# Reordering the second, third and fourth head groups of a fused attention and maxout kernel: loads, casts, masks and value products

## The chip, the cores and the metric

The kernel runs on one core of one Trainium2 chip. A core has five engines that run side by side, each through its own queue in order: TensorE (PE, matrix products; its weight loads are shown as PEld), VectorE (DVE), ScalarE (ACT), GpSimd (POOL) and SyncE (SP). SP, ACT and POOL also issue DMA transfers; those that POOL issues go through one queue (q0, "software"), those of SP through another (q1). The metric is the time of one execution on the device, in microseconds (us); lower is better. Seven runs of the kernel before the change gave a median of 258.22 us, from 257.61 to 260.21.

## What is computed

Blockwise causal attention feeds a maxout layer.

```python
B, H, S, D = 8, 8, 576, 64; block = 64
scores = (q @ k.transpose(0, 1, 3, 2)) / sqrt(D)
scores = where(block_i >= block_j, scores, -1e9)     # by blocks of 64 positions
attn = softmax(scores)
x = (attn @ v).transpose(0, 2, 1, 3).reshape(4608, 512)
g = maximum(x @ w1, x @ w2)                          # w1, w2: 512 x 1024
out = g @ w_out                                      # w_out: 1024 x 512
```

All inputs and the output are float32; the kernel works in bf16 with float32 accumulation.

## The kernel before

**Pairs and groups.** Two heads with the same place in their pair of heads are handled together as a *pair* p (32 pairs, four to a batch), since 64 rows of head dimension fill half of TensorE's rows. Two pairs make a *group* g (16 groups, two to a batch). Groups 0 and 1 are a hand-written start with their own tiling; group 2 is written out by hand too; groups 3 to 15 run in a loop. The change touches group 2 and the first turns of the loop (groups 3 and 4).

**One group.** `load_qk` brings q and k of the group as float32 (SP issues the DMA; a one-element memset on POOL, the "gate", stands before it and holds it until POOL gets there). `cast` turns them into bf16. `transposes` turns them on TensorE into PSUM and returns a function that copies the result out (two copies, one for each pair, on the engines named). `pad_keys` (POOL) prepares a copy of some keys for the corner blocks. Then for each pair three tiles of scores: `tile_0`, `tile_1`, `tile_2` write scores into one of two PSUM buffers (`ps_s`), and return a function that takes the exponential on ACT (1024 columns each, tile_2 with a small second one) into `aT` and sets the masked corners to zero with memsets on POOL (`mask`). `region` calls these functions. With two buffers, the scores of a tile wait for the exponential of the tile before the last one.

**Values.** `av(p, ts)` multiplies the exponentials of a pair with V (`ps_o`), and DVE divides by the sums (reciprocal and multiply) into `xp`. `av_with(p, n)` does it in two parts with n steps of other work between. V of a batch comes in five chunks, `load_v(b, c)`, issued by POOL. `x_out(g)` transposes a group's values into `xT` (two copies); for groups from 4 on a DMA does this instead. When the second group of a batch is through, `done_tokens` rises, and more of the second layer may run.

**The second layer.** max(x w1, x w2) is computed as max(x (w1 - w2), 0) + x w2. `diff_w(j)` is the subtraction for a quarter of the columns on DVE (it needs `load_w1(j)`, 512 KB, and `load_w2(j)`, both issued by POOL). The second part times w_out is one matrix, M = w2 w_out, which the kernel computes itself (`bT_unit`, `m_unit`). `h_unit(i, f)` is one block of 128 hidden columns for a span of 512 tokens (four matmuls, then DVE's maximum with 0 into `g`); columns f = 0 and 1 need `diff_w(0)`, 2 and 3 `diff_w(1)`, and so on. `y_unit` makes 128 rows of output (twelve matmuls, a DVE copy, a store by SP).

**Fill.** All these are units in one list, and `fill(n)` puts the next n steps of them (a 512-column matmul is one step, a 256-column one a half) into TensorE's queue between the parts of attention. `fill_of(g)` says how many steps a group gets: what is ready, less KEEP = 14, divided by the groups left until more becomes ready.

**What sets the order.** Every engine runs its instructions in the order in which the program writes them; there is no scheduler. Four PSUM buffers (`ps_m`) serve transposes, M, h, y and the values; two (`ps_s`) the scores. Raw q and k have three buffers each, the bf16 copies two, `aT` four (one a pair). `pool_work(s)` is called at the end of a pair's turn in the loop: the loads of the group after next but one, the casts of the group after next, the V chunks of the next batch.

**Around the change, in the order written (line numbers of the kernel before):** the second part of the start issues `load_w1(0)` and the load of group 2 (625, 626), `load_w1(1)`, `load_w1(2)` (636, 637), `load_w1(3)` (646), the casts of group 2 and the load of group 3 (647 to 649) and V's first chunk (650); group 2 is transposed (656, 657), scored (663, 667, 671) and masked tile by tile, with the other V chunks and `diff_w` between; then come the casts of group 3 (673, 674), its transposes (679, 682), and the loads of groups 4 and 5 with the casts of group 4 (`pool_work(4)`, `pool_work(5)`). In the loop the values of pair p - 2 run in the turn of pair p.

Of the kernel before, what the change touches and what calls it, by code (L numbers as in the profile page):

```python
# [14 lines left out]
def kernel(  # L15
# [12 lines left out]
    B, H, S, D = q.shape  # L28
    P = 128
    BLK = 64  # L30
    HP = H // 2
# [367 lines left out]
    def exp(p, ps, w, a0):  # L399
        nc.scalar.activation(  # L400
            out=aT_r[p % NA][:, :, a0:a0 + w], in_=ps[:, :, :w], func=AF.Exp, scale=scale,
        )
# [36 lines left out]
    def tile_0(p):  # L439
        u = ps_s.tile([P, 2, 512], FP32, name="ps_s", tag="s")  # L440
        scores(p, u, 0, 0, 0, 512)
        return lambda: (exp(p, u, 512, 0), mask(p, 0))

    def tile_1(p):
        u = ps_s.tile([P, 2, 512], FP32, name="ps_s", tag="s")
        scores(p, u, 0, 0, 512, 64)
        scores(p, u, 64, 1, 128, 448)
        return lambda: (exp(p, u, 512, 512), mask(p, 576))

    def tile_2(p):  # L450
        u = ps_s.tile([P, 2, 512], FP32, name="ps_s", tag="s")
        corner_scores(p, u, 320)
        scores(p, u, 0, 2, 256, 320)
        scores(p, u, 384, 3, 448, P)

        def out():
            exp(p, u, 512, 1024)
            nc.scalar.activation(  # L458
                out=aT_r[p % NA][BLK:, :, 1536:AW], in_=u[BLK:, :, 320:320 + BLK],
                func=AF.Exp, scale=scale,  # L460
            )
            mask(p, 1024)
            mask(p, 1344)
        return out

    def region(*tiles):
        for out in tiles:
            out()

    def av(p, ts):  # L470
        b, hp = divmod(p, HP)
# [75 lines left out]

    def pool_work(s):
        g, i = divmod(s, 2)
        if s == 4:  # L550
            load_qk(4, (SP, SP), gated=True)
        elif s == 5:
            load_qk(5, (SP, SP), gated=True)
            cast("q", 4, ((pool, 0, RPP),))
            cast("k", 4, ((pool, 0, RPP),))
        else:
            if i == 1 and g + 3 < NG:
                load_qk(g + 3, (SP, SP), gated=True)
            if i == 1 and g + 2 < NG:
                cast("q", g + 2, ((pool, 0, RPP),))  # L560
                cast("k", g + 2, ((pool, 0, RPP),))
            nb, j = divmod(s + 2, HP)
            if nb < B:
                for c in ((0, 1), (2, 3), (4,), ())[j]:
                    load_v(nb, c)
            for nm in "qk":
                if i == 1 and g + 3 < NG and by_dma(nm, g + 3):
                    load_blocks(nm, g + 3)
# [65 lines left out]
    burst_q3(2)  # L634
    masks_q(2)
    load_w1(1)
    load_w1(2)
    fill(2)
    burst_q1(3)
    fill(2)  # L640
# [2 lines left out]
    av(2, [2, 3, 4])  # L643
    burst_q3(3)
    masks_q(3)
    load_w1(3)
    cast("q", 2, ((pool, 0, RPP),))
    load_qk(3, (SP, SP), gated=True)
    cast("k", 2, ((pool, 0, RPP),))
# [4 lines left out]
    x_out(1, 0, NCH, (act, act))  # L654
    fill(4)
    transposes("q", 2, (dve, act))()
    transposes("k", 2, (dve, act))()
    pad_keys(4)
    pad_keys(5)
    load_v(1, 1)  # L660
    diff_w(0)
    fill(4)
    region(tile_0(4), tile_1(4))
    load_v(1, 2)
    load_v(1, 3)
# [100 lines left out]
```

## Time and profile before

| | us |
|---|---|
| median of 7 runs | 258.22 |
| lowest, highest | 257.61, 260.21 |
| the profiled execution, whole | 259.17 |
| its span, first to last instruction | 257.4 |
| TensorE busy | 241.0 (94%) |
| DVE, POOL, ACT busy | 149.5, 124.5, 119.5 |

Busy time by stretch, us (from 23 to 26: end of the start; 30.5 to 45.7: group 2; then groups 3 and 4, and group 5's first part):

| stretch | length | TensorE | DVE | ACT | POOL |
|---|---|---|---|---|---|
| 23.0 to 26.0 | 3.0 | 0.61 | 0.82 | 0.85 | 1.15 |
| 26.0 to 30.5 | 4.5 | 4.50 | 2.03 | 0.81 | 3.20 |
| 30.5 to 45.7 | 15.2 | 13.82 | 11.73 | 10.31 | 9.95 |
| 45.7 to 54.6 | 8.9 | 8.55 | 5.91 | 6.35 | 5.39 |
| 54.6 to 64.4 | 9.8 | 8.65 | 5.41 | 7.73 | 9.07 |
| 64.4 to 78.0 | 13.6 | 12.70 | 9.12 | 8.03 | 10.38 |

TensorE's clock was granted in full (0.999) over the whole span. In rows of the instructions in order of time, the first number is the start, the second the duration, both in us; "x16" is the number of instructions merged, and the bracket the engine's idle time ahead of the row and what released it. The end of a matmul is modelled, so a hole in TensorE's work is best read from start to start.

### The profile page before, as it was taken

What the parts mean: (1) busy time and instruction counts of PE and PEld (TensorE: products, weight loads), DVE (VectorE), ACT (ScalarE), POOL (GpSimd) and SP (SyncE); (2) the same over time, 40 slices, a digit from 0 to 9 for tenths busy, and PEclk for the clock granted to TensorE, in tenths of its full rate; (3) what the DMA queues carried; (4) which work ended last, traced back from release to release, by engine and by line L of the source; (5) the groups of instructions that cost most, each with busy time, mean ns of one, the idle gap of its engine ahead of it and who ended that gap; (6) DMA issues with size and microseconds to landing.
All of it is one profiled execution on the core that took longest, in us unless ns stands there. A gap on an engine that the chain in (4) does not pass through costs nothing.

```text
span 257.4 us, 6711 instructions
## 1 busy us (share of the span) xinstructions
PE 241.0 (94%) x2733; PEld 132.7 (52%) x2768; DVE 149.5 (58%) x300; ACT 119.5 (46%) x159; POOL 124.5 (48%) x289
## 2 busy tenths in 40 slices
PE   7796998989899999999999999999999999999994
PEld 2364853546555555555555555555545564444443
DVE  4976559656576447644764575457535754753521
ACT  2876384687664655555555556464646400000000
POOL 2984496569958456845685568557331100000000
PEclk9999999999999999999999999999999999999999
DMA  7999999979999999999999999999961312111122
GB/s 245 214 157 254 339 310 70 362 52 218 187 170 194 153 210 162 221 154 224 144 222 155 217 147 204 164 213 155 122 127 59 92 43 81 43 39 45 72 91 83
DMA packets 104383, 41.27 MB, mean 160 GB/s; under 512 B 89248, under 2 KB 93728, under 8 KB 104352
## 3 DMA queue, kind: packets, MB, share of 16 engines
q0 software_dynamic: 65952, 11.87, 61.1%
q1 hardware_dynamic: 37984, 28.32, 47.7%
q10 hardware_dynamic: 416, 0.66, 0.7%
q8 instruction: 21, 0.34, 0.6%
q14 instruction: 10, 0.08, 0.1%
HBM read 34.60 MB, written 9.44 MB: 171 GB/s over the span
## 4 chain that ended last, share of the span: by engine, by line
PE 80%; DMA 6%; POOL 4%; ACT 4%; issue 3%; DVE 1%; ACTq 0%; POOLq 0%
PE ps_y L268 34%; PE ps_h L226 23%; PE ps_o L486 10%; PE ps_s L376 7%; DMA wo_sb<-in_moe_w_out_dram 4%; ACT aT L400 2%; PE ps_qT L357 2%; DMA qraw<-in_q_dram 2%; PE ps_M L249 2%; POOL vv L159 2%; POOL xT L180 1%; PE ps_y L283 1%; POOL qn L155 1%; PE ps_s L394 1%; POOL aT L405 1%
## 5 line engine op out<-in xcount | busy, mean ns | idle before, releaser
L400 ACT ACTIVATE aT<-ps_s 128x1024 bf16<-128x1024 f32 (+2 forms) x100 | 95.8, 994 | 43.9 <-PE ps_s L376 32.9
L268 PE MATMUL ps_y<-wo_sb,g 128*128 128x512 bf16 x260 | 66.5, 379 | 3.1 <-issue 3.0
L226 PE MATMUL ps_h<-xT,d_sb 128*128 128x512 bf16 x278 | 67.2, 380 | 0.7 <-issue 0.2
L231 DVE TENSOR_SCALAR g<-ps_h 128x512 bf16<-128x512 f32 x72 | 49.6, 690 | 20.5 <-PE ps_h L226 20.4
L405 POOL MEMSET aT<- 64x128 bf16 x128 | 23.0, 202 | 64.6 <-ACT aT L400 63.7
L273 DVE COPY y<-ps_y 128x512 f32<-128x512 f32 x35 | 24.2, 692 | 45.5 <-PE ps_y L268 44.7
L486 PEld LDWEIGHTS <-aT 128*128 128x128 bf16 x960 | 37.4, 98 | 14.0 <-issue 0.7
L226 PEld LDWEIGHTS <-d_sb 128*128 128x128 bf16 x288 | 26.5, 98 | 31.2 <-issue 2.6
L268 PEld LDWEIGHTS <-g 128*128 128x128 bf16 x280 | 24.7, 98 | 30.3 <-issue 5.7
L486 PE MATMUL ps_o<-vv,aT 128*128 128x65 bf16 x960 | 39.7, 194 | 0.0
L268 PE MATMUL ps_y<-m_sb,xT 128*128 128x512 bf16 x137 | 37.8, 379 | 0.1
L159 POOL DMA_DIRECT2D vv<-in_v_dram x40 | 34.0, 855 | 0.9 <-issue 0.5
L376 PE MATMUL ps_s<-qT,kT 64*128 64x128 bf16 (+6 forms) x344 | 31.6, 281 | 3.0 <-ACT aT L458 1.5
L493 DVE TENSOR_TENSOR xp<-ps_o,rec 128x256 bf16<-128x256 f32 (+1 forms) x64 | 31.4, 491 | 2.2
L132 POOL DMA_DIRECT2D kb<-in_k_dram x40 | 29.4, 760 | 0.0
L492 DVE RECIPROCAL rec<-ps_o 128x4 f32<-128x4 f32 (+1 forms) x64 | 11.9, 187 | 23.1 <-PE ps_o L486 22.8
L288 ACT COPY y<-ps_y 128x256 f32<-128x256 f32 (+1 forms) x2 | 0.6, 320 | 49.3 <-PE ps_y L283 49.3
L365 ACT COPY qT<-ps_qT 128x576 bf16<-128x576 bf16 x15 | 9.6, 639 | 26.3 <-PE ps_qT L357 26.3
L155 POOL CAST qn<-qraw 128x1152 bf16<-128x1152 f32 (+1 forms) x15 | 17.1, 1140 | 6.8 <-DMA qraw<-in_q_dram 5.7
L268 PEld LDWEIGHTS <-xT 128*128 128x128 bf16 x140 | 12.8, 98 | 13.5 <-issue 0.5
L376 PEld LDWEIGHTS <-kT 64*128 64x128 bf16 x344 | 11.9, 94 | 14.1 <-issue 9.2
L365 DVE COPY qT<-ps_qT 128x576 bf16<-128x576 bf16 x17 | 12.8, 750 | 0.6 <-PE ps_qT L357 0.6
(58 smaller groups left out, 136.5 us busy)
## 6 DMA issues: line engine op xcount, KB each, us to landing
qraw<-in_q_dram SPq DMA_DIRECT2D x16, 576.0 KB, 4.8
out_dram<-y SPq DMA_DIRECT2D x35, 256.0 KB, 4.0
vv<-in_v_dram POOLq DMA_DIRECT2D x32, 128.0 KB, 5.7
kraw<-in_k_dram SPq DMA_DIRECT2D x5, 576.0 KB, 7.5
kb<-in_k_dram POOLq DMA_DIRECT2D x40, 72.0 KB, 6.8
w1raw<-in_moe_w_dram POOLq DMA_DIRECT2D x4, 512.0 KB, 13.5
xT<-in_moe_w_dram POOLq DMA_DIRECT2D x4, 256.0 KB, 6.8
wo_sb<-in_moe_w_out_dram POOLq DMA_DIRECT2D x2, 512.0 KB, 12.4
```

The source lines that it names most:

```text
L132: nc.gpsimd.dma_start(out=n[h * BLK:(h + 1) * BLK, :, s], in_=(q if nm == "q" else k)[b, 4 * u + 2 * s + h].rearrange("(j p) d -> p j d", ...
L159: nc.gpsimd.dma_start(out=vv_r[b % NV][P - rows:, c, :, :D], in_=v[b, :, c * P:c * P + rows, :].rearrange("h p d -> p h d"),)
L226: nc.tensor.matmul(pt[:], d_sb[:, c, f * P:(f + 1) * P], xT[:, c, t0:t0 + SPAN], start=(c == 0), stop=(c == NDM - 1),)
L231: nc.vector.tensor_scalar_max(g[:, f], pt[:], 0.0)
L268: nc.tensor.matmul(py[:], lhs, rhs, start=(n == 0), stop=(n == len(terms) - 1),)
L273: nc.vector.tensor_copy(out=y[:], in_=py[:])
L365: (copy or copies[i])(out=t[:, p0 * RPP:p1 * RPP].rearrange("q (p j) -> q p j", j=RPP), in_=pts[i][:, :, p0:p1].rearrange("q j p -> q p j"),)
L376: nc.tensor.matmul(ps[:, hh, col:col + w], kT[r, k0:k0 + P], qT[r, q0:q0 + w], start=True, stop=True,)
L400: nc.scalar.activation(out=aT_r[p % NA][:, :, a0:a0 + w], in_=ps[:, :, :w], func=AF.Exp, scale=scale,)
L405: (eng or nc.gpsimd).memset(aT_r[p % NA][BLK:, :, a0:a0 + BLK], 0.0)
L486: nc.tensor.matmul(po[:, gi, hh, :], a[:, hh, a0:a0 + P], vv[:, c, h0 + 2 * hh, :], start=(mm == 0), stop=(mm == n_mm - 1),)
L493: nc.vector.tensor_mul(xp[:, :, ts[0]:ts[0] + n, p % 2].rearrange("q s t d -> q t s d"), po[:, :, :, :D], rec[:, :n].to_broadcast([P, n, 2 ...
```

## The change

- `load_w1(2)` and `load_w1(3)` leave the start. Block 2 is issued after group 2's `pad_keys`, block 3 after V's fourth chunk.
- Five fill steps go between group 2's q and k transposes, three (not four) behind them.
- Group 2's eight masks are taken out of the tiles (`masked=False`) and issued together after its last exponential.
- Group 3's q is cast on POOL ahead of the V chunks, its k on DVE behind `diff_w(1)`. Its q is transposed before the last two tiles of group 2, its k after the next four fill steps and `diff_w(2)`, with both copies on DVE.
- The loads of group 4 are issued in the middle of group 2, those of group 5 at its end, where also group 4's casts stand; `pool_work` loses its special cases. The fill of `fill_of(2)` is replaced by fixed steps.
- `diff_w(3)` moves into the turn of pair 6. The values of pair 6 come at the end of group 3 and those of pair 7 in the turn of pair 8; in the turn of pair 9 `x_out(3)` takes the place of values and raises `done_tokens`; group 5 then begins without an `x_out`.

```diff
     def tile_0(p):
...
-        return lambda: (exp(p, u, 512, 0), mask(p, 0))
+        return lambda masked: (exp(p, u, 512, 0), masked and mask(p, 0))
...
-    def region(*tiles):
+    def region(*tiles, masked=True):
         for out in tiles:
-            out()
+            out(masked)
...
     def pool_work(s):
         g, i = divmod(s, 2)
-        if s == 4:
-            load_qk(4, (SP, SP), gated=True)
-        elif s == 5:
-            load_qk(5, (SP, SP), gated=True)
-            cast("q", 4, ((pool, 0, RPP),))
-            cast("k", 4, ((pool, 0, RPP),))
-        else:
...
     load_w1(1)
-    load_w1(2)
...
     masks_q(3)
-    load_w1(3)
     cast("q", 2, ((pool, 0, RPP),))
     load_qk(3, (SP, SP), gated=True)
     cast("k", 2, ((pool, 0, RPP),))
...
     transposes("q", 2, (dve, act))()
+    fill(5)
     transposes("k", 2, (dve, act))()
+    load_v(1, 1)
     pad_keys(4)
     pad_keys(5)
-    load_v(1, 1)
+    load_w1(2)
     diff_w(0)
-    fill(4)
-    region(tile_0(4), tile_1(4))
+    fill(3)
+    region(tile_0(4), tile_1(4), masked=False)
+    cast("q", 3, ((pool, 0, RPP),))
     load_v(1, 2)
     load_v(1, 3)
+    load_w1(3)
+    load_v(1, 4)
+    load_qk(4, (SP, SP), gated=True)
+    diff_w(1)
+    cast("k", 3, ((dve, 0, RPP),))
     fill(8)
-    region(tile_2(4), tile_0(5))
-    load_v(1, 4)
-    diff_w(1)
+    region(tile_2(4), tile_0(5), masked=False)
     fill(8)
-    region(tile_1(5), tile_2(5))
+    copy_out = transposes("q", 3, (dve, act))
+    outs = tile_1(5), tile_2(5)
+    copy_out()
+    region(*outs, masked=False)
+    for p in (4, 5):
+        for a0 in (0, 576, 1024, 1344):
+            mask(p, a0)
+    fill(4)
     diff_w(2)
-    cast("q", 3, ((pool, 0, RPP),))
-    cast("k", 3, ((pool, 0, RPP),))
-    fill(4)
-    diff_w(3)
-    n = fill_of(GPB)
-    fill(n // 2)
-    transposes("q", 3, (dve, act))()
-    pool_work(4)
-    fill(n // 3)
-    transposes("k", 3, (dve, act))()
+    transposes("k", 3, (dve, dve))()
     pad_keys(6)
     pad_keys(7)
-    pool_work(5)
-    fill(n - n // 2 - n // 3)
+    load_qk(5, (SP, SP), gated=True)
+    cast("q", 4, ((pool, 0, RPP),))
+    cast("k", 4, ((pool, 0, RPP),))
+    fill(4)
 
     for g in range(GPB + 1, NG):
...
             done_tokens[0] = old if p == a and x_by_dma(g - 2) else new
+            if p == 6:
+                diff_w(3)
             fill(hi)
-            av_with(p - LAG, lo)
+            if p == 9:
+                x_out(3)
+                new = done_tokens[0]
+            else:
+                av_with(p - 1 if p == 8 else p - LAG, lo)
...
-        x_due.append(g - 1)
+        if g != GPB + 2:
+            x_due.append(g - 1)
         fill(n - 2 * (lo + hi))
+        if g == GPB + 1:
+            av_with(6, lo)
```

More of the change, by code (lines that the diff above doesn't have):

```diff
@@ L447, in tile_1 @@
         scores(p, u, 64, 1, 128, 448)
-        return lambda: (exp(p, u, 512, 512), mask(p, 576))
+        return lambda masked: (exp(p, u, 512, 512), masked and mask(p, 576))
     def tile_2(p):
@@ L454, in tile_2, with out @@
         scores(p, u, 384, 3, 448, P)
-        def out():
+        def out(masked):
             exp(p, u, 512, 1024)
@@ L461, in out @@
             )
-            mask(p, 1024)
-            mask(p, 1344)
+            if masked:
+                mask(p, 1024)
+                mask(p, 1344)
         return out
-    def region(*tiles):
+    def region(*tiles, masked=True):
         for out in tiles:
-            out()
+            out(masked)
     def av(p, ts):
@@ L549, in pool_work @@
         g, i = divmod(s, 2)
-        if s == 4:
-            load_qk(4, (SP, SP), gated=True)
-        elif s == 5:
-            load_qk(5, (SP, SP), gated=True)
-            cast("q", 4, ((pool, 0, RPP),))
-            cast("k", 4, ((pool, 0, RPP),))
-        else:
[L557 to L568, printed above, removed]
+        if i == 1 and g + 3 < NG:
+            load_qk(g + 3, (SP, SP), gated=True)
+        if i == 1 and g + 2 < NG:
+            cast("q", g + 2, ((pool, 0, RPP),))
+            cast("k", g + 2, ((pool, 0, RPP),))
+        nb, j = divmod(s + 2, HP)
+        if nb < B:
+            for c in ((0, 1), (2, 3), (4,), ())[j]:
+                load_v(nb, c)
+        for nm in "qk":
+            if i == 1 and g + 3 < NG and by_dma(nm, g + 3):
+                load_blocks(nm, g + 3)
     T_AT = {s: [("qk"[s % 2], s // 2 + 1)] for s in range(NPAIR - 2)}
```

## The prediction

> **What bounds the kernel now.** I read the page first, for the busy shares and the slices, then TensorE's instructions in order of time between 20 and 70 us, and for each hole the other engines' instructions in that stretch.
>
> ```profile
> span 257.4 us, 6711 instructions
> PE 241.0 (94%) x2733; PEld 132.7 (52%) x2768; DVE 149.5 (58%) x300; ACT 119.5 (46%) x159; POOL 124.5 (48%) x289
> PE   7796998989899999999999999999999999999994
> ```
>
> TensorE sets the time: 94% busy, in the nines from slice 12 on, clock full. The change leaves the number of matmuls as it is, so it can win only holes in TensorE's row, and lose only by new ones. The span has 1.8 us around it in this execution (259.17 in all); the median of the runs is 258.22, so I make the sum against 257.4 + 1.8 and take the difference off the median.
>
> ```profile
> 25.70 1.92 PE L249 MATMUL ps_M<-wo_sb,bT_sb 128*128 128x256 bf16 x16 [2.39 <-DMA wo_sb<-in_moe_w_out_dram]
> ...
> 31.82 1.03 PE L249 MATMUL ps_M<-wo_sb,bT_sb 128*128 128x256 bf16 x8 [0.25 <-ACT qT L365]
> ...
> 38.49 3.20 PE L226 MATMUL ps_h<-xT,d_sb 128*128 128x512 bf16 x14
> 42.44 0.44 PE L357 MATMUL ps_qT<-ident,qn 64*128 64x64 bf16 x18 [0.76 <-POOL qn L155]
> ...
> 55.88 0.40 PE L376 MATMUL ps_s<-qT,kT 64*128 64x64 bf16 x4 [0.82 <-ACT aT L458]
> ...
> 65.50 0.40 PE L376 MATMUL ps_s<-qT,kT 64*128 64x64 bf16 x4 [0.69 <-ACT aT L458]
> ```
>
> The bracket is TensorE's idle time before the row and what ended it. The 2.39 us before 25.70 wait for w_out and lie ahead of all that is edited; the new program issues w_out at the same place, so they stay. Behind that, from start to start less 0.216 us for each 512-column matmul (the chain of waits has 36 of them in 7.77 us at 243.26) and half of it for 256 columns, the holes are: 0.25 at 31.82; 0.24 before h's first matmul at 36.85; 0.30 before 38.13; 0.93 before group 3's q transposes (38.49 + 14 x 0.216 = 41.51, next start 42.44); 0.33 and 0.29 in rows up to 45.73; then 1.0 and 0.86 at the first scores of groups 4 and 5. Together **4.2 us**: this is all there is to win.
>
> ```profile
> 40.24 0.34 POOL L405 MEMSET aT<- 64x128 bf16 x2 [0.72 <-ACT aT L400]
> 40.65 1.74 POOL L155 CAST qn<-qraw 128x1152 bf16<-128x1152 f32 x1
> 42.34 1.14 POOL L155 CAST kn<-kraw 128x1152 bf16<-128x1152 f32 x1
> ```
>
> This is why the 0.93 arises: q of group 3 landed at 37.8 (issued 27.29, 10.5 us), but its cast stands behind masks that wait for the last exps, and then takes 1.74 us instead of 1.14, because DVE's subtraction runs beside it:
>
> ```profile
> 32.37 2.44 DVE L183 TENSOR_TENSOR d_sb<-w1raw,xT 128x1024 bf16<-128x1024 f32 x2
> ...
> 40.17 1.22 DVE L183 TENSOR_TENSOR d_sb<-w1raw,xT 128x1024 bf16<-128x1024 f32 x1
> ```
>
> **The change part by part.**
>
> *Fewer bytes ahead of group 3's q, k.* Two w1 blocks (1 MB) leave POOL's queue at 22.2 and 24.2. By the DMA view POOL's queue moved 1.11 MB alone between 28 and 31, and 0.63 MB beside 0.45 MB of q, k between 32 and 35; without the blocks only two V chunks stand there. Beside V packets q, k got 0.25 MB in the one us from 36, so q, in motion from 31 on, lands near 34, k near 36, instead of 37.8 and 39.5 (27.76 + 11.7). Nothing is won by that alone; it feeds the next step.
>
> *Group 2's front.* Five fill steps now stand between the q and the k transposes: 1.08 us of M matmuls that cover the copies of q, so the 0.25 goes. The k copies end some 1.1 us later: kT(4) on DVE from 32.5 takes 0.75, TensorE has matmuls until 33.1: a new wait of **0.2**. DVE then subtracts blocks 0 and 1, 33.25 to 35.6. POOL's pad_keys, which took 2.45 us beside such a pair (32.52, twice 0.26 elsewhere), ends again only with it, at 35.7; the corner scores need it at 35.65: **0.1**.
>
> *Casts of group 3.* q on POOL: behind pads (35.95) and the issue of w1 block 2 (0.75), 36.7 to 37.85; its transposes are due at 38.05. No wait, with 0.2 us of cover: each us of POOL later costs one. k on DVE, 1.34 us (row of the first cast there, 128x1152), 35.7 to 37.0 where POOL took 1.14; hidden, since DVE next waits for the first h unit, which ends at 37.2. The 0.93, 0.24, 0.30, 0.33 go with this.
>
> [...] The five V issues from 6.18 to 10.5 took 4.33 us, 0.87 each, while DVE ran four such fp32 casts, against a mean of 0.855 over all forty: no slowing. [...]
>
> *Group 2's tail.* Thirteen fill steps (2.8 us) move out of group 2 into groups 3 and 4; total work is the same. TensorE's rows from 33.3: scores 0.6, M 1.73, scores 0.65, h 1.73, q transposes 0.4, scores 0.6, h 0.86, k transposes 0.4, h 0.86, so group 3 could start at 41.3. But DVE's order is now: g of the third h unit (due 40.05), subtraction of block 2, then both k copies. 40.05 + 0.62 + 1.2 + 0.7 = 42.55: the first scores of group 3 wait **1.2** us. This is the new wait that takes the place of the old one; the queue behind it is DVE's: second k copy, g, subtraction 3, g, values. Bounds: 0.7 if g and copies overlap as pipelined rows do, 2.2 if block 2 (issued 35.95) lands at 41.7 rather than before 40.7; a 512 KB block took 12.0 to 13.9 us in a full queue, 576 KB in an idle one 3.7 (43.54). The queue is nearly idle then, so I take 4.
>
> *Masks in one go.* Eight masks at 0.17 to 0.20 on POOL after the V chunks, w1 block 3 and the loads of group 4: from 41.1, done by 42.4 for pairs 4 and 5. Their first reader, the values of pair 4, comes at 44.3. Free; without that cover, 1.4.
>
> *Groups 4 and 5 sooner.* POOL: w1 block 2 from 35.95 (0.75), cast 1.14, two V chunks 0.87 each, block 3 0.75, last V chunk 0.69: 41.1. SP then issues group 4's q, k at 41.2 and 41.6 instead of 43.54 and 44.01, beside block 3 and V in the other queue; q lands near 45.2 (3.7 alone), is cast by 46.4 to 46.8. Its transposes are due at 42.5 + 0.6 + 1.08 + 0.2 + 0.65 + 0.73 = 45.8; they need also DVE's g of the fifth h unit and the values' first multiply, behind subtraction 3: k copy 43.2, g 43.9, subtraction 45.1, g 45.7, values 46.3. Wait **0.6**; bounds 0 (everything lands early) and 2. Group 5's load follows at 43.7 instead of 46.33; no other transfer stands behind it until 56.
>
> *Values of pair 6 at group 3's end, of pair 7 in pair 8's place, x_out(3) within group 4.* In group 3 28 fill steps instead of 19 and 0.95 us of values stand before group 4's first scores, after the last exps (2.25 us): the hole of 1.0 goes. Group 4 keeps 19 steps but has values of one pair only, so ACT presses: x_out(3)'s copies and ACT's exps make the second half wait **0.35**, and group 5's first scores wait for the last exp **0.4** instead of 0.86, since 8 steps (1.73) instead of 5 cover it.
>
> New waits: 0.2 + 0.1 + 1.2 + 0.6 + 0.35 + 0.4 = 2.85. Won: 4.2 - 2.85 = **1.4 us**: span 256.0, this execution 257.8, median 256.8. From group 6 on both have the same fill left (KEEP, 14), and TensorE is dense in both.
>
> **The rivals.**
>
> *Slower: DVE stands at subtraction 3.* It is placed ahead of every g and value copy of group 3, and block 3 goes out only at 39.6. DVE is free for it at 43.9; each us that the block lands later is paid in full, as TensorE has four m-buffers. The V chunks issued into a filled queue at 36 to 38 took 6.0 to 7.1 us. At 7.1 plus 0.8 of issue the block lands at 47.4: 3.5 us, 260.3. It turns the sign beyond 45.3, and makes over 0.5% beyond 46.6. Against it: the queue ahead holds 256 KB then, not 1.5 MB. A second way to this side is that the change doesn't do what it says: if q, k land at 37.8 and 39.5 as before, DVE waits with the k cast until 39.5, three us with h's copies behind it: 259.8.
>
> *No change: the wait only moves.* The 1.2 is 1.7 and the 0.6 is 1.4 (DVE is the busiest engine there: 4.62 of 5 us between 40 and 45 already before): 258.1.
>
> *More.* The copies overlap, block 3 and q land early, and ACT's two waits are covered: 0.2 + 0.1 + 0.9 + 0.3 + 0.1 left, 2.6 won: 255.6.
>
> **How the numbers follow.** The forecast (256.8; own range 256.2 to 257.4) 0.5, no change 0.15, more 0.15, slower 0.2 (block 3 late 0.15, q, k no sooner 0.05). About 0.5%, 1.3 us, is what a measurement of this kernel tells from no change: the line is 256.9. Of the forecast's half 0.35 lies under it. Faster 0.35 + 0.15 = 0.5, same 0.15 + 0.15 = 0.3, slower 0.2. The range leaves out a tenth at each end: 255.3 to 259.4.
>
> **What would show it.** Right: group 3's q cast on POOL before 38 and no POOL wait at its transposes; the first scores of group 3 near 42.5, waiting for a DVE kT copy right behind a subtraction; group 4's first scores without an ACT wait; 65 us for group 5's first scores in place of 65.5, with three fill steps less before it. Wrong: a wait of DVE on w1's landing, q, k of group 3 landing after 36.5, or a hole of over 1.5 us at group 4's q transposes.

## The result and the profile after

The changed kernel took 261.81 us (median of 27 runs, 259.39 to 265.71); the kernel before took 258.53 in the same comparison. The ratio is 1.0095, with a 95% interval of 1.0071 to 1.0119: slower by 1%, where 0.5% faster was forecast. The ratio leaves out executions over 1.5% above the fastest of the same kernel, so that here and in the table below it is not the quotient of the two medians. The profiled execution took 262.4 us.

One thing is needed to read the times below: TensorE's clock is halved for a while in some executions. In the profiled one it was granted at 0.50 for 3.41 us (49.66 to 53.07, last section); that lowers the mean of 261 us by 0.007, and its mean is 0.993. How many such stretches another execution had is an estimate from its mean granted clock, in steps of 0.007. By it, of 28 executions of the changed kernel 7 had none (median 259.66), 15 had one (261.88), 6 more (263.75). Of 134 executions of the kernel before, run beside the experiments below, 87 had none (258.33), 39 one (260.72), 8 more (263.31). So the change costs two things: 1.3 us at full clock (0.8 to 1.5 by the comparison that the kernel before is taken from), and at least one half-clock stretch in 21 of 28 executions instead of 47 of 134. "At full clock" below means the median of the executions with a mean clock of 0.996 or more.

The page of the changed kernel: span, busy times, TensorE's busy tenths in 40 slices, its granted clock.

```profile
span 260.6 us, 6715 instructions
PE 242.8 (93%) x2732; PEld 133.5 (51%) x2768; DVE 151.7 (58%) x302; ACT 119.0 (46%) x158; POOL 122.8 (47%) x288
PE   8797997598999999999999999999999999999994
PEclk9999999899999999999999999999999999999999
```

The span is 3.2 us longer. In slices 7 and 8 (39.1 to 52.1 us) TensorE is busy for 7 and 5 tenths, where it was 8 and 9, and in the eighth its clock dips. TensorE's instructions in order of time there (start, duration, and in the bracket the idle time and what ended it):

```profile
42.30 0.61 PE L376 MATMUL ps_s<-qT,kT 64*128 64x512 bf16 x6 [1.30 <-DVE kT L365]
...
44.76 0.71 PE L487 MATMUL ps_o<-vv,aT 128*128 128x65 bf16 x18
46.47 0.34 PE L487 MATMUL ps_o<-vv,aT 128*128 128x65 bf16 x6 [1.00 <-DMA vv<-in_v_dram]
48.93 0.44 PE L357 MATMUL ps_qT<-ident,qn 64*128 64x64 bf16 x18 [2.12 <-POOL qn L155]
...
49.81 0.61 PE L226 MATMUL ps_h<-xT,d_sb 128*128 128x512 bf16 x1
50.63 1.48 PE L226 MATMUL ps_h<-xT,d_sb 128*128 128x512 bf16 x3 [0.22 <-issue]
```

Group 3 starts at 42.30 instead of 45.73. Then the values of pair 4 wait for V's last chunk, and group 4's q transposes for the cast of a q that has only just landed. From start to start, less the modelled time of the matmuls between, the two holes are 1.17 and 2.29 us. From the last row to the next, at 51.91, three of h's matmuls start 0.43 us apart, twice 0.216: the half clock. The same place in the kernel before:

```profile
47.98 0.89 PE L486 MATMUL ps_o<-vv,aT 128*128 128x65 bf16 x24
48.80 0.44 PE L357 MATMUL ps_qT<-ident,qn 64*128 64x64 bf16 x18
```

Group 4's q transposes start at 48.80 there, without a wait, and at 48.93 here. The 3.4 us by which group 3 came sooner are gone at this row; but the 13 fill steps that left group 2 are not done yet (group 3 has done 8 steps by then, 7 before). TensorE stands 12 steps, 2.6 us, behind.

What VectorE and GpSimd (POOL) did meanwhile in the changed kernel, first VectorE:

```profile
41.48 1.42 DVE L365 COPY kT<-ps_kT 128x576 bf16<-128x576 bf16 x2
42.82 0.68 DVE L231 TENSOR_SCALAR g<-ps_h 128x512 bf16<-128x512 f32 x1
45.87 1.23 DVE L183 TENSOR_TENSOR d_sb<-w1raw,xT 128x1024 bf16<-128x1024 f32 x1 [2.37 <-DMA w1raw<-in_moe_w_dram]
```

```profile
37.02 1.76 POOL L159 DMA_DIRECT2D vv<-in_v_dram  x2
38.76 0.79 POOL L177 DMA_DIRECT2D w1raw<-in_moe_w_dram  x1
39.52 0.72 POOL L159 DMA_DIRECT2D vv<-in_v_dram  x1
...
47.73 1.14 POOL L155 CAST qn<-qraw 128x1152 bf16<-128x1152 f32 x1 [4.38 <-DMA qraw<-in_q_dram]
49.23 1.15 POOL L155 CAST kn<-kraw 128x1152 bf16<-128x1152 f32 x1 [0.36 <-DMA kraw<-in_k_dram]
```

Three engines wait for transfers at once. Block 3 of w1, issued at 38.76, is there at 45.8 (7.0 us); V's last chunk, issued at 39.52, at 46.4 (6.9); group 4's q, issued at 40.37, at 47.7 (7.3). In the kernel before, q was issued 3.2 us later, at 43.54, and was there at 47.2, sooner. The DMA view of the kernel before from 40 to 44 us says why (busy tenths of the 16 DMA engines in 40 slices of 0.1 us; GB/s; packets by size; POOL's queue with its packets, MB and their time as a share of the 16 engines' time; the load issued there, with its us to landing):

```profile
DMA  9999999999999999999999959976423220000000
GB/s 127 127 132 137 212 124 96 82 73 69 38 31 42 40 36 32 28 27 33 33 22 27 30 27 37 27 22 19 17 10 9 8 6 0 0 0 0 0 0 0
DMA packets 1362, 0.18 MB, mean 45 GB/s; under 512 B 1361, under 2 KB 1361, under 8 KB 1361
q0 software_dynamic: 1361, 0.17, 119.1%
qraw<-in_q_dram SPq DMA_DIRECT2D x1, 576.0 KB, 3.7
```

The bytes look like an idle queue, 127 GB/s falling to 20. The engines were full until 42.5, with V's packets of under 512 B, and empty from 43.3. Group 4's q was issued into that gap. The changed kernel, same stretch:

```profile
DMA  9999999999998994869959799799999999999999
q0 software_dynamic: 1757, 0.71, 125.0%
q1 hardware_dynamic: 48, 0.11, 16.2%
qraw<-in_q_dram SPq DMA_DIRECT2D x2, 576.0 KB, 7.3
```

There is no gap: POOL's queue (q0) moves 0.71 MB instead of 0.17, and SP's queue (q1), which carries q and k, moves 0.11 MB though both loads of group 4 were issued by 40.84. (The second load of q in the last line is group 5's.)

### The profile page after: what moved, and what is told of

Same layout as the page of the kernel before. It is cut to its first block, busy times and chain, and to the rows that moved or that the text cites. A ratio compares the mean times of both kernels' runs of the same rounds, so it can differ in the third digit from the quotient of the medians.

```text
span 260.6 us, 6715 instructions
## 1 busy us (share of the span) xinstructions
PE 242.8 (93%) x2732; PEld 133.5 (51%) x2768; DVE 151.7 (58%) x302; ACT 119.0 (46%) x158; POOL 122.8 (47%) x288
## 4 chain that ended last, share of the span: by engine, by line
PE 79%; DMA 9%; POOL 6%; issue 2%; ACT 2%; DVE 0%; ACTq 0%; POOLq 0%; DVEq 0%
PE ps_y L268 34%; PE ps_h L226 23%; PE ps_o L487 10%; PE ps_s L376 7%; DMA qraw<-in_q_dram 5%; DMA wo_sb<-in_moe_w_out_dram 4%; POOL vv L159 2%; PE ps_M L249 2%; PE ps_qT L357 2%; ACT aT L400 1%; POOL xT L180 1%; POOL qn L155 1%; PE ps_y L283 1%; POOL kz L383 1%; PE ps_s L394 1%
## 5 line engine op out<-in xcount | busy, mean ns | idle before, releaser
L226 PE MATMUL ps_h<-xT,d_sb 128*128 128x512 bf16 x277 | 68.5, 385 | 1.2 <-issue 0.7
L273 DVE COPY y<-ps_y 128x512 f32<-128x512 f32 x35 | 24.2, 692 | 47.7 <-PE ps_y L268 46.9
L487 PE MATMUL ps_o<-vv,aT 128*128 128x65 bf16 x960 | 40.2, 194 | 1.3 <-DMA vv<-in_v_dram 1.3
L155 POOL CAST qn<-qraw 128x1152 bf16<-128x1152 f32 (+1 forms) x15 | 16.5, 1101 | 11.2 <-DMA qraw<-in_q_dram 11.2
```

The lines of the kernel that those rows point to most:

```text
L226: nc.tensor.matmul(pt[:], d_sb[:, c, f * P:(f + 1) * P], xT[:, c, t0:t0 + SPAN], start=(c == 0), stop=(c == NDM - 1),)
L273: nc.vector.tensor_copy(out=y[:], in_=py[:])
L487: nc.tensor.matmul(po[:, gi, hh, :], a[:, hh, a0:a0 + P], vv[:, c, h0 + 2 * hh, :], start=(mm == 0), stop=(mm == n_mm - 1),)
```

## The experiments

Eighteen kernels were run. The theory: the front of this kernel is bound by transfers up to about 47 us. The change pulls the work that needs them forward, takes away the fill that covered their landing, and puts 1 MB of w1 beside V and group 4's q; the half clock follows from the holes. The rivals: VectorE's early subtraction holds group 4 up (the rival named in the prediction); the order of the transfers is wrong, not their amount; one separate part (the masks, the loop) does the harm.

In the last column, two rows of different comparisons can differ by 0.7 us without a cause in the kernel: the kernel before has medians at full clock of 258.14 to 258.84 in the six comparisons.

| run | edit | us (before beside it) | ratio, 95% interval | at full clock |
|---|---|---|---|---|
| changed kernel | | 261.81 (258.53) | 1.0095 [1.0071, 1.0119] | 259.66 |
| e1 | subtraction 3 a pair later | 264.17 (258.94) | 1.0209 [1.0140, 1.0278] | none |
| e2 | e1, group 4's q, k first | 262.13 (258.94) | 1.0101 [1.0039, 1.0163] | 261.12 (of two) |
| e3 | w1 blocks back at the start | 260.90 (258.94) | 1.0051 [1.0016, 1.0086] | 260.78 |
| e6 | w1 blocks ahead of V | 259.53 (258.46) | 1.0032 [0.9996, 1.0068] | 259.13 |
| e9 | 8 fill steps back | 262.63 (258.92) | 1.0138 [1.0083, 1.0193] | none |
| e10 | e9 + e6, group 4's q, k sooner | 259.77 (258.92) | 1.0059 [1.0015, 1.0103] | 259.60 |
| e7 | e6, group 3's k cast on POOL, subtraction 2 sooner, group 4's q, k sooner | 260.31 (258.46) | 1.0066 [1.0032, 1.0100] | 259.53 |
| e13 | block 3's transfer left out | 259.03 (258.74) | 1.0009 [0.9972, 1.0045] | 258.44 |
| e14 | 13 zero matmuls added | 260.50 (258.74) | 1.0079 [1.0041, 1.0118] | 260.26 |
| e16 | two V chunks left out | 261.93 (258.43) | 1.0102 [1.0017, 1.0187] | 259.22 and 262.17 |
| e17 | both left out | 257.73 (258.43) | 0.9963 [0.9927, 0.9998] | 257.74 |
| e18 | e6, group 5's load later | 259.20 (258.86) | 1.0017 [0.9982, 1.0052] | 259.19 |
| e4 | before + the loop's part alone | 260.08 (258.94) | 1.0022 [0.9978, 1.0067] | 259.14 |
| e8 | before + masks in one go alone | 259.81 (258.46) | 1.0024 [0.9982, 1.0067] | 259.13 |
| e11 | e8, subtraction 3 after q | 260.03 (258.92) | 1.0043 [1.0003, 1.0083] | 258.98 |
| e12 | before, group 2's load later | 266.11 (258.92) | 1.0287 [1.0238, 1.0335] | none |
| e5 | 10 zero matmuls in the hole | 261.08 (258.46) | 1.0114 [1.0049, 1.0180] | 260.85 |
| e15 | before + 8 zero matmuls | 259.17 (258.74) | 1.0023 [0.9992, 1.0054] | 259.16 |

### Is it the subtraction? (e1, e2)

```diff
-            if p == 6:
+            if p == 7:
                 diff_w(3)
```

> The changed kernel with diff_w(3) in the turn of pair 7 instead of pair 6, nothing else. Landing theory (the holes at group 3's values and group 4's q transposes, 1.2 and 2.3 us in the profile after, come from transfers that land late: V's last chunk 46.4, q of group 4 47.7): those transposes still start at 48 to 49, since q still lands near 47.7, and the time is within 1 us of the changed kernel (about 261). DVE theory (the subtraction that stands on DVE until w1's block 3 has landed at 45.9 holds up g and the values): the transposes start near 46.5, no row at half clock follows, and the time falls by 2 to 4 us to 258 to 259.

TensorE in e1:

```profile
48.55 0.44 PE L357 MATMUL ps_qT<-ident,qn 64*128 64x64 bf16 x18 [2.21 <-POOL qn L155]
...
51.15 1.46 PE L226 MATMUL ps_h<-xT,d_sb 128*128 128x512 bf16 x3 [1.69 <-DVE d_sb L183]
```

VectorE stands nowhere before group 4's q transposes now, and the hole there is as long (2.38 from start to start); the q landed at 47.3. The subtraction, one pair later, adds a second hole. So the rival of the prediction is not the cause: it waits for the same thing as the others. e2 keeps that edit and also moves group 4's load ahead of group 3's q cast and V's last chunk ahead of block 3:

```diff
+    load_qk(4, (SP, SP), gated=True)
     cast("q", 3, ((pool, 0, RPP),))
     load_v(1, 2)
     load_v(1, 3)
+    load_v(1, 4)
     load_w1(3)
-    load_v(1, 4)
-    load_qk(4, (SP, SP), gated=True)
```

> As the run before, and besides group 4's q, k are loaded ahead of group 3's q cast (issue near 36 instead of 40.4), and V's last chunk goes ahead of w1's block 3. Landing theory: q of group 4 lands by 43 to 44, V's last chunk by 44, both holes go, TensorE's clock stays full, and the time falls to 256.5 to 258. DVE theory: no gain over the run before. A third reading, that the DMA engines are simply full between 31 and 46: q lands by 44 but V or block 3 takes its place and a hole of 1 to 2 us stays.

```profile
45.72 0.43 PE L487 MATMUL ps_o<-vv,aT 128*128 128x65 bf16 x9 [0.95 <-DMA vv<-in_v_dram]
46.40 0.34 PE L487 MATMUL ps_o<-vv,aT 128*128 128x65 bf16 x6 [0.24 <-DMA vv<-in_v_dram]
46.67 0.43 PE L357 MATMUL ps_qT<-ident,qn 64*128 64x64 bf16 x18
...
49.41 1.87 PE L226 MATMUL ps_h<-xT,d_sb 128*128 128x512 bf16 x5 [1.84 <-DVE d_sb L183]
```

The q transposes come at 46.67 without a wait. V's chunks are late instead (1.12 and 0.40 from start to start), and the next h unit waits 2.0 for the subtraction of block 3, which stands behind the late values on VectorE. The holes together are as long as before. Another order gives the waiting to another reader.

### Other orders, and the fill put back (e3, e6, e7, e9, e10)

e3 issues both w1 blocks at the start, where the kernel before has them. e6 puts them ahead of V's chunks:

```diff
+    load_w1(2)
     load_v(1, 1)
     pad_keys(4)
     pad_keys(5)
-    load_w1(2)
+    load_w1(3)
...
-    load_w1(3)
     load_v(1, 4)
```

> The changed kernel with w1's blocks 2 and 3 issued at the start, where they were before. Landing theory: q, k of group 3 land at 37.8 and 39.5 again, so the k cast on DVE (and h's copies behind it) wait to 39.5 and cost 2 to 3 us in group 2; V's last chunk, block 3 and group 4's q land early and the holes of 1.2 and 2.3 us and the half clock go: 257.5 to 260. If the two blocks' place has no part in the holes, they stay and the time is 261 to 264.

> The changed kernel with w1's block 2 issued ahead of V's second chunk and pad_keys (near 32 instead of 35.2) and block 3 right behind pad_keys (near 36 instead of 38.8). Queue theory (pad_keys holds POOL up for 2.4 us behind the subtraction, so the DMA engines run half empty from 35 to 38 and everything behind lands late): block 3 lands by 41, V's last chunk by 44 and q of group 4 by 46, so the holes of 1.2 and 2.3 us shrink to under 1.5 together, and the time falls by 2 to 4 us to 258 to 260. If the engines are full by bytes alone: q, k of group 3 land 2 us later instead, and the time stays at 261.

In e3 V and block 3 are in time and the hole at the q transposes shrinks to 0.52 (49.43), but the first scores of group 3 start at 45.73, 3.4 later than in the changed kernel: 1.8 of it comes from a longer hole at w_out (3.38 in this profile), the rest is the half-clock stretch that follows there, from 28.2 to 31.6 (mean granted clock of the profile 0.993). Group 3's k is cast on VectorE only from 39.39 (36.63), as was expected of the late landing, but TensorE does not wait for it. Why e3 is at 260.78 at full clock, the profile of an execution with half clock does not show. In e6 V is in time, and the q transposes wait 2.36 as before; of the orders tried it costs least, 259.13 at full clock, 0.8 to 0.9 above the kernel before. e7 and e10 build on e6:

> As the run before, and besides k of group 3 cast on POOL again, diff_w(2) ahead of group 3's q transposes on DVE, group 4's load ahead of both casts. Queue theory and my DVE term together: the 1.3 us hole at group 3's first scores shrinks to about 0.4, q of group 4 lands by 44, no hole over 1 us is left behind 26, and the time is 256.5 to 257.5. If V's chunks, now last, are late: a hole of 1 to 2 us at the values of pair 4 and 258 to 260.

> As the run before, with w1's block 2 ahead of V's second chunk, block 3 behind pad_keys, and group 4's load ahead of V's last chunks. Deadline theory: nothing over 1 us is left behind 27 but ACT's waits at groups 4 and 5: 257.5 to 258.5, even with the kernel before or better. If bytes are still short, V's last chunk comes late and a hole of 1 to 2 us stays: 259 to 260.

e7 won the first scores of group 3 (hole of 0.41 instead of 1.47) and the q transposes, and lost 1.84 and 0.91 at V. e9 and e10 put eight fill steps back behind group 2:

```diff
     cast("k", 4, ((pool, 0, RPP),))
-    fill(4)
+    fill(12)
```

> The changed kernel with eight of the thirteen fill steps put back at the end of group 2 (fill(12) in place of the last fill(4)); the transfers are issued as in the changed kernel. Deadline theory (the transfers can't land before 45 to 48 in any order, and the thirteen steps that left group 2 were the work that covered them): group 3 starts near 42.8 without the 1.3 us wait, its q transposes are due 1.7 us later, the holes of 1.2 and 2.3 us shrink to 0 and 0.5 to 1, and the time falls by 2 us or more to about 259.5. If the holes have another cause they stay, and the time is 261 to 262.

Neither is a clean test of the cover: the fill is taken from one list in order, so that the steps that need block 3 came forward with it, and waited for it (3.23 us at 51.25 in e9, 1.98 at 45.60 in e10).

### Less to move, or more cover (e13, e14)

e13 leaves out the transfer of block 3 (its quarter of w1 is made from block 2's raw columns); e14 adds thirteen matmuls on zeros, 2.8 us, where the fill stood.

```diff
-    load_w1(3)
+    w1_raw[3] = w1_raw[2]
```

> The changed kernel without the transfer of w1's block 3 (512 KB less; the fourth quarter of w1 - w2 uses block 2 in its place, so that quarter is left out of the result). Landing theory, by bytes: V's last chunk and group 4's q land 1 to 2 us sooner (by 45 and 46), the subtraction no longer waits, the holes of 1.2 and 2.3 us shrink to 0.5 to 1.5 together, the half clock goes in most runs, and the time falls by 2 to 4 us to 258 to 259.5. If it is latency from the issue and not bytes: q of group 4 still lands 7 us after its issue, the hole at its transposes stays over 1.5 us, and the time is 260 to 261.5.

> The changed kernel with thirteen matmuls of zeros (2.8 us, results unused) at the end of group 2, where thirteen fill steps were taken out; no transfer and no other order is touched. Deadline theory (the transfers land when they land, and the steps that left were their cover): group 3's first scores move by 1.5 us only (the DVE wait of 1.3 goes), the holes of 1.2 and 2.3 us shrink by as much, the half clock goes, and the time stays between 259.5 and 261.5 although 2.8 us of work were added. If the holes hang on TensorE's own order, the time rises by 2.8 us to 264 to 265.

TensorE in e13, then in e14:

```profile
44.67 0.89 PE L487 MATMUL ps_o<-vv,aT 128*128 128x65 bf16 x24
47.26 0.44 PE L357 MATMUL ps_qT<-ident,qn 64*128 64x64 bf16 x18 [1.70 <-POOL qn L155]
```

```profile
40.97 2.97 PE L687 MATMUL ps_s<-zeros 128*128 128x512 bf16 x13
...
49.17 0.44 PE L357 MATMUL ps_qT<-ident,qn 64*128 64x64 bf16 x18 [1.95 <-POOL qn L155]
```

Without 512 KB (e13) the hole at V is gone, q is there 1.7 us sooner, and the loss is gone: 258.44 at full clock, as before the change. In e14 2.8 us of work that does nothing were added; the holes at the first scores and at V are gone, and the q transposes start at 49.17 instead of 48.93. At full clock it costs about 0.6 of its 2.8 us; the median over all executions even came out 1.3 lower than the changed kernel's, since 8 of 12 executions kept the clock. TensorE had that time to spare: what it does before 47 us doesn't set when it goes on. This is the clearest evidence for the theory.

### Bytes, packets, or neighbours in the queue (e16, e17, e18)

q still took 6.2 us in e13, against 3.7 before. e16 leaves out V's third and fourth chunk (the values read the second in their place) and keeps block 3; masks that nobody reads hold POOL for as long as their issue did (1.81 us for 1.76). e17 leaves out both.

```diff
...
-    load_v(1, 2)
-    load_v(1, 3)
+    for a0 in (0, 576, 1024, 1344) * 3:
+        mask(6, a0)
```

> The changed kernel without V's third and fourth chunk of the second batch (256 KB, 2048 of the packets under 512 B); where they were issued GpSimd sets masks that nobody reads, twelve at 0.15 us, so that all behind them is issued when it was; batch 1's values read V's second chunk in place of the two. Block 3 of w1 stays. Theory that the engines' time counts, of which V's small packets take most: V's last chunk, block 3 and group 4's q land 1.5 to 2 us sooner than in the changed kernel (46.4, 45.8, 47.7), more than without block 3's 512 KB (q 46.1): q near 45.9, hole at V gone, hole at group 4's q transposes 1.2 to 1.8, no half clock behind it in most executions; 258 to 259. Theory that bytes count: 256 KB are half of block 3's, so q lands near 46.9, 260 to 261. Theory that engines, not transfers, hold group 4's q: nothing moves, 261 to 262.

> As the one before, and block 3 of w1 left out too (its quarter uses block 2's raw columns): of the transfers beside group 4's q only 192 KB of V are left. It tests the rest of the prediction's sum, with the term that failed taken away. If the rest was right: group 4's q lands 3.7 to 4.5 us after its issue at 40.4, that is by 45, its transposes follow the values of pair 4 with a hole of at most 0.6, the kernel takes 256.8 to 257.4 at full clock, faster than the kernel before. If the landings only uncover another wait (VectorE's subtraction, copies and values, 4.5 of 5 us busy between 39 and 44): the hole stays at 1 or more, 258 and over.

In e16 V's last chunk and block 3 were in time (VectorE subtracts at 43.59 without a wait), as the theory of the packets had it, but q landed at 47.3, 0.35 sooner only, which none of the three readings had: 45.9 by the packets, 46.9 by the bytes, and in the third V and block 3 should not have moved either. Its four executions had mean clocks from 0.987 to 1.0, so its time tells nothing. In e17 q is there when POOL is free for it, at 43.47 or before, at most 4.5 us after its issue at 39.02. So it is not V's packets alone nor block 3 alone that holds q; either is enough. That SP's queue gets little done while POOL's has much to move would explain it (0.11 MB beside 0.71 in the view above), but was not tested by itself. The rows of e17 that decide its time, on TensorE, POOL and VectorE:

```profile
46.35 0.19 PE L357 MATMUL ps_qT<-ident,qn 64*128 64x64 bf16 x1 [0.52 <-DVE g L231]
46.91 0.43 PE L357 MATMUL ps_qT<-ident,qn 64*128 64x64 bf16 x17 [0.36 <-DVE xp L494]
```

```profile
43.47 1.16 POOL L155 CAST qn<-qraw 128x1152 bf16<-128x1152 f32 x1
44.85 1.86 POOL L155 CAST kn<-kraw 128x1152 bf16<-128x1152 f32 x1 [0.23 <-DMA kraw<-in_k_dram]
```

```profile
43.61 2.09 DVE L183 TENSOR_TENSOR d_sb<-w1raw,xT 128x1024 bf16<-128x1024 f32 x1
```

With the transfers gone the transposes wait for VectorE, 1.20 in all, as the subtraction takes 2.09 beside POOL's casts instead of 1.22. That is the second reading that was written down for e17, of a hole of 1 or more, though its time of 258 and over did not come: at 257.74 the kernel is 0.6 faster at full clock than the kernel before in all comparisons, 0.4 than beside it (ratio 0.9963, upper end 0.9998), all ten executions without half clock. But it leaves out work that the kernel needs.

The last run tried another neighbour: group 5's load, which the change also issues sooner.

> The changed kernel with the order of e6 (blocks 2 and 3 of w1 ahead of V's second chunk and right behind the padded keys: no hole at V, hole of 2.36 at group 4's q transposes, 259.53), and group 5's load behind the casts of group 4 instead of ahead of them. In e6 SP's queue had moved some 1.4 MB when group 4's q (576 KB) was there at 49.08, since group 4's k and, from 45.8, group 5's q and k are in motion beside it. Theory that transfers of one queue share the engines and do not follow each other: with group 4's two alone about 1.0 MB (as without V's chunks and block 3, where q was there after 1.0 MB) goes ahead, q lands 1.0 to 1.2 sooner, hole 1.2 to 1.4, 258.3 to 258.8 in executions at full clock, where e6 took 259.1. Theory that group 5's load has no part: hole 2.2 to 2.5, 259.1 at full clock and 259.5 over all. Group 5's own q, k then land near 55 and are cast at 58: no new wait expected.

q of group 4 was there 6.4 us after its issue (6.7 in e6), and the hole is 2.05 instead of 2.36: group 5's load has at most a small part in it (the profile of e6 is one with a half-clock stretch, earlier), and the time, 259.19 at full clock, did not move. Why q takes 6 us from issue even without block 3, with V's last three chunks issued ahead of it (e13), stays open.

### Single parts in the kernel before (e4, e8, e11, e12)

```diff
...
-            av_with(p - LAG, lo)
+            if p == 9:
+                x_out(3)
+                new = done_tokens[0]
+            else:
+                av_with(p - 1 if p == 8 else p - LAG, lo)
...
```

> The kernel before with the loop's part of the change alone (values of pair 6 at group 3's end, of pair 7 in pair 8's turn, x_out(3) in pair 9's). My prediction's terms for this part: the waits of 1.0 and 0.86 at groups 4 and 5 shrink to 0.4 and 0.5, gain 0.5 to 1 us, 257.5. If this part is what made the changed kernel slow: 259 or more.

The loop's part alone changes nothing that can be told (259.14 at full clock against 258.84 beside it, ratio 1.0022). Group 4's first scores wait no longer; group 5's still wait 0.99, and the second half of group 4's k transposes 0.72. e8 takes group 2's masks behind group 3's casts:

> The kernel before with group 2's masks alone taken out of the tiles and put behind group 3's casts. My reading of the profile before (the 0.93 us hole at 41.5 comes from the q cast standing behind masks on POOL): the q cast starts near 39.2 instead of 40.65, the hole goes, gain 0.5 to 0.9 us: 258.0. If q's landing (37.8) or the subtraction beside the cast decides, no gain: 258.9.

q was cast 3.2 us sooner, and the hole at its transposes grew from 0.93 to 1.49. VectorE, POOL and TensorE in e8:

```profile
37.61 2.08 DVE L183 TENSOR_TENSOR d_sb<-w1raw,xT 128x1024 bf16<-128x1024 f32 x1
...
40.22 1.56 DVE L183 TENSOR_TENSOR d_sb<-w1raw,xT 128x1024 bf16<-128x1024 f32 x1
```

```profile
37.47 1.15 POOL L155 CAST qn<-qraw 128x1152 bf16<-128x1152 f32 x1 [0.92 <-DMA qraw<-in_q_dram]
39.32 1.38 POOL L155 CAST kn<-kraw 128x1152 bf16<-128x1152 f32 x1 [0.70 <-DMA kraw<-in_k_dram]
```

```profile
42.43 0.42 PE L357 MATMUL ps_qT<-ident,qn 64*128 64x64 bf16 x17 [1.32 <-DVE g L231]
```

Each cast now lies beside a subtraction and stretches it (2.08 and 1.56 us, where 1.22 was measured in the kernel before); g comes late, and with it the PSUM buffer that the transposes need. So the reading in the prediction that the masks ahead of POOL's cast make the 0.93 fell: with them away, VectorE makes 1.49.

e11 moved `diff_w(3)` behind group 3's q transposes: a hole of 0.36 there, and one of 0.97 behind the k transposes (44.65). "Lock" in its expectation is a name for the longer times measured in e8; no run shows the mechanism.

> The masks-only kernel (e8) with diff_w(3) behind group 3's q transposes. In e8 the hole at 41 stayed (1.5 us), now waiting for g on DVE, whose two subtractions took 2.08 and 1.56 us beside POOL's casts instead of 1.22. If that lock is the cause: the hole goes, and the time is 257.5 to 258 (0.5 to 0.9 us under the kernel before). If not, the hole stays: 258.5 to 260.

> The kernel before with group 2's load issued behind its masks (near 21.5 instead of 18.9), away from w_out's first half. If q, k of group 2 are what slows w_out (from 22.4 they took 250 KB/us and left it 57): w_out lands near 24, the hole of 2.4 us at 23.3 shrinks by 1 to 2 us, but q of group 2 lands near 28.5 and costs up to 1 us at its transposes: 257.5 to 258.5. If the engines give w_out no more without them: 259 to 260.

e12 shows the same one stage earlier. With group 2's load issued behind its masks, w_out comes in time and its hole is gone; group 2's q and k come late, 3.54 and 3.62 us, and the clock is halved for 10 us from 30.4 (mean granted clock of the profile 0.978).

### The clock (e5, e15)

> The changed kernel with ten matmuls of zeros (2.2 us, results unused) on TensorE ahead of group 4's q transposes, where it otherwise stands idle for q. Clock theory (the hole itself costs its length, and the half clock that follows it from 49.7 for 3.4 us costs another 1.7 us): the transposes start where they did (48 to 49), no row at half clock follows in most runs, and the time falls from 261.8 to about 260. If the half clock has another cause, it stays and the time is 261 to 262.5.

> The kernel before with eight matmuls of zeros (1.7 us, results unused) in the hole of 2.4 us ahead of w_out. Clock theory (runs of the kernel before at 0.99 of the clock are runs in which that hole was long enough for a half-clock stretch of 3.4 us): fewer runs at 0.99, the median falls by 0.2 to 0.5 us, the fastest runs stay at 257.5 to 258. If the half clock comes from elsewhere, its share stays near a third, and the time is the same or 1 us longer where w_out lands early.

Zeros in the hole at group 4's q transposes (e5) take the half clock away from there (granted 1.00 from 49 to 54 us, 0.66 in the changed kernel), and 4 of 6 executions kept the clock (7 of 28 without them), but the profile had a stretch from 25.73, after a hole of 2.46 at w_out (mean granted clock 0.993), and at full clock the kernel is 1.2 slower than without them. In the kernel before, zeros in the hole at w_out (e15) kept the clock in all 12 executions (87 of 134 without them); they cost 0.7 to 0.8 at full clock, so that the median is no better.

No version beat the kernel before with all of its work done.

## Why the prediction was wrong, step by step

- **Group 3's q, k sooner**: right. They landed at 34.95 and 36.5 (34 and 36 forecast); POOL's cast started at 35.93, VectorE's at 36.63, and the transposes at 37.56 had no wait. Two V issues took 1.76 beside VectorE's cast, 0.88 each, as the rows had it that the forecast went by (0.87 each).
- **Group 2's front**: waits of 0.33 and 0.32 for 0.2 and 0.1.
- **First scores of group 3**: forecast at 42.5 with a wait of 1.2 for the k copy behind a subtraction; 42.30, and 1.30 in the bracket (1.47 from start to start). That the start fits so well is partly luck: the new waits up to here were 2.12 for 1.5, while the hole at w_out, which the prediction left at 2.39, was 1.41 in this profile. Block 2 took 5.0 us from its issue instead of 4, but was issued 0.8 sooner than forecast, so that it was there at 40.2, when VectorE came to it (40.35).
- **Masks in one go**: free, done at 41.6.
- **Landings at group 4: the step that failed.** "The queue is nearly idle then, so I take 4" and "q lands near 45.2" were read from the bytes that stood in the queue and from a 3.7 us transfer that had run in the one gap there was. In the kernel before the engines were full of V's small packets until 42.5, and the change itself filled the gap. Block 3 took 7.0 us, q 7.3, V's last chunk, whose landing was not costed at all, 6.9. The term of 0.6 (bounds 0 and 2) measured 1.17 + 2.29 = 3.46 in the profile, 2.86 more. That the forecast (256.8) and the time at full clock (259.66) also lie 2.86 apart is chance: the other new waits came out 0.87 longer than forecast, the hole at w_out 1.0 shorter, and the profiled execution had a half-clock stretch. For those at full clock there is an estimate: from group 4's q transposes to the end of the span it is 210.0 us in e13 and 210.2 in e18, both without half clock; the seven executions of the changed kernel at full clock have a median span of 257.9, which puts the transposes near 47.9, 1 us sooner than in the profile. If all of that is less waiting, about 2.4 of the 3.46 are left there, four times the 0.6.
- **What takes the cover away** was written down in the same text, but only as "total work is the same": the thirteen steps that left group 2 were the work that hid these landings. e14 showed that work put back in their place costs little there, about 0.6 of 2.8 us.
- **The rival "VectorE stands at subtraction 3"** had the place and half of the mechanism: the block landed at 45.8, past its sign point of 45.3, and VectorE waited 2.37, which with the hole of 2.29 makes two of the three signs of being wrong. e1 showed that it decides nothing by itself.
- **Groups 4 and 5**: group 4's first scores wait no more, right; the second half waits 0.72 for 0.35, group 5's first scores 0.28 for 0.4.
- **The half clock** was not foreseen: executions with one stretch take 2.2 us more (261.88 less 259.66), of which 3.41 us at half the clock are 1.7. At full clock the time (259.66) is just past the range's end of 259.4; the half clock carries the median to 261.81.

e17 tests the rest of the sum with the failed term's cause removed: 0.4 to 0.6 faster at full clock, not 1.4. It still holds 1.20 at group 4's q transposes (0.6 forecast), 1.47 at the first scores (1.2) and 0.72 (0.35), 1.2 us more than forecast, more than the 0.8 to 1.0 that is missing.

## What to carry to other kernels

Work that stands between the issue of a transfer and its reader is a cover: before it is moved, look up when each transfer behind it lands, and by what the DMA engines are busy, not by how many bytes are queued (in the kernel before they were 9 tenths busy from 40 to 42.3 us while the rate fell from 127 to 30 GB/s). A landing time measured in a gap holds only as long as the gap does (3.7 us for q of group 4 before, 7.3 after). And where a stretch is bound by transfers, another order mostly changes who waits: e2 and e7 each cured one hole and got another, and the best order, e6, still stood 0.8 us above the kernel before at full clock.

## What was not expected of the hardware

**Half clock followed holes of 1.17 and 2.29 us.** The windows of the changed kernel, then of the kernel before (us, length, busy time and count on the five engines, granted clock, DMA share, GB/s):

```profile
44.00:49.00 5.00, 1.88 (x40) 1.31 (x40) 3.06 (x7) 0.75 (x1) 1.14 (x1) 1.00 1.04 342
49.00:54.00 5.00, 4.78 (x64) 2.60 (x66) 3.00 (x6) 2.86 (x4) 2.93 (x8) 0.66 0.31 116
```

```profile
44.00:49.00 5.00, 4.89 (x81) 2.69 (x81) 3.60 (x8) 2.58 (x3) 1.89 (x6) 1.00 0.86 297
49.00:54.00 5.00, 4.68 (x97) 2.95 (x90) 3.62 (x9) 3.81 (x6) 2.90 (x8) 1.00 0.48 180
```

TensorE was busy for 1.88 of 5 us, in holes of 1.17 and 2.29 with 0.3 us of matmuls between; the granted clock of the next 5 us is 0.66, which is 3.4 us at half (by slices of 0.25 us, from 49.66 to 53.07: 3.41). Holes that together make 2.75 us or more were followed by half clock in the profiles of the changed kernel, e1, e2 (0.66 from 49 to 54 in all three) and e7 (mean 0.993); a single one of 2.1 was in e14 (0.66 there too), of 2.36 was not in e6 (the five matmuls of h behind it took 1.25 us, 1.87 in e14), nor of 2.05 in e18 (mean 1.0). So length alone does not decide, and 7 of 28 executions of the changed kernel had no stretch. What decides is not shown. That the holes are the cause is supported by taking them away: with zeros in the hole at w_out (e15) all 12 executions kept the clock, and with the two holes of 3.46 cut to 1.20 (e17) all ten.

**VectorE's subtraction and POOL's casts and key copies held each other up; VectorE's cast held nothing up in the rows read.** Beside two subtractions (2.44 us from 32.62) POOL's padded keys took 2.45 us (0.52 elsewhere), and beside POOL's casts the subtraction took 2.08, 1.56 (e8) and 2.09 (e17) instead of 1.22. In these rows the one that started first kept its time: in the kernel before the subtraction started at 40.17 and took 1.22, POOL's cast at 40.65 took 1.74 instead of 1.14; in e8 the cast started at 37.47 and took 1.15, the subtraction at 37.61 took 2.08. Beside VectorE's cast in the changed kernel (36.63, 1.35 us) POOL's cast took 1.16 (1.14 elsewhere) and two V issues 0.88 each (median of forty in the kernel before 0.885). Why the two kinds differ, no run shows.
